# A gated mix of a recurrent-memory attention and a GEGLU block: an eviction, one shared weight slot and the order of some loads are moved

## The chip, the cores and the metric

The kernel runs on one core of one Trainium2 chip. The metric is the device time of one execution in microseconds. A core has five engines that work side by side, each on its own list in order: TensorE (PE, matmuls; its weight loads are shown as PEld), VectorE (DVE), ScalarE (ACT), GpSimd (POOL) and SyncE (SP, which here only issues DMAs). DMA transfers run on 16 DMA engines that all queues share: what SP issues goes through queue q1, what POOL issues through q0, what ACT issues through q10. Matmuls write to eight PSUM banks; ACT or DVE must copy ("evict") a bank to SBUF before its content can be used by PE again.

## The reference

The input x has 2048 rows of 1024. One half (A) is an attention with a recurrent memory: x is cut into 64 segments of 32 rows, and each segment is preceded by 8 memory rows, which are the output of the segment before at its first 8 positions. The other half (B) is a GEGLU block. A gate per row mixes both.

```python
for s in range(n_seg):                       # 64 segments, one after the other
    h = concat([mem, x[:, 32*s:32*s+32]])    # 8 + 32 rows of 1024
    q, k, v = h @ Wq, h @ Wk, h @ Wv         # 32 heads of 128
    p = softmax(where(mask, q @ k.T * scale, -1e9))
    o = (p @ v) @ Wo                         # back to 1024
    mem = o[:, :8]; outs.append(o[:, 8:])
a = concat(outs)
b = (gelu(x @ w_gate) * (x @ w_up)) @ w_down # hidden size 3584
g = sigmoid((x * gate_w).sum(-1))
out = g * a + (1 - g) * b
```

The segments cannot run side by side, since each needs the memory rows of the one before.

## The kernel before, in words

The work is written down once as a list of operations, each with its engine and the tiles it reads and writes; a small class (`_Prog`) works out the semaphore waits from overlaps of these tiles in SBUF and PSUM. So each engine's order is the order in which the operations are listed, and two tiles that lie on the same SBUF bytes make their users wait for one another.

**Weights.** Wq, Wk, Wv and Wo are cut into two halves of 16 heads (u = 0, 1) and eight pieces (i = 0 to 7) of 512 KB each: 64 pieces. SBUF has room for 50 slots. `PAIRS` (L313) names the pieces for which both halves share one slot: two of Wk, two of Wq, four of Wv and six of Wo. A shared slot is loaded anew in each segment. A segment works with one half first (r = 0) and with the other then (r = 1), and the next segment starts with the half that the last one ended with, so a shared slot is loaded once per segment: `spent` (L405) issues the load of the other half from SP as soon as a piece has been used at r = 0. `firsts` (L508) issues the first loads of a half in segment 0. `seq` (L315) gives the order in which the pieces of a half are used. Wo is first read in the layout of the input; as `keep` (L380) it is copied, piece by piece in the first segments, to a scratch tensor wo_scr (one copy per segment, L879), from which later loads come (`load_piece`, L374).

**One segment.** The order of the projections is written out in `HEAD` and `BODY` (L322, L323): first half of Wk, Wq (with the second four steps of the last segment's second Wo half, `("o", 1, 4, 8)`, between them) and Wv; then the second half of Wk and Wq; then Wo at r = 0; then the second half of Wv, then the first four steps of Wo at r = 1. Every projection has eight steps, one piece each (`proj`, L708; Wk, Wq, Wv are the matmuls of L719, Wo at r = 0 those of L735, Wo at r = 1 those of L752). Everything else is hung on these steps by `plan` (L848): `on(m, r, n, f)` lists f just ahead of step n of projection (m, r).

**What hangs there.** `evac` copies a full bank to a stage tile (L613 to L617): kS and qS for the first Wk half and for Wq, pS for the second Wk half. `trans` (L635) turns a stage over with PE transposes (L631) and a DVE copy. `scores` (L644) makes the scores (L647, L653) and the softmax (DVE L659, L660, ACT exponential E of L661, DVE L663 to L672; the last one is the transpose to the tile tAB). `attend` (L674) multiplies the result tAB with the values: the tile vA, evicted from the Wv bank, and vB, read back from a scratch tensor (PE L681, L686). `take` evicts the result to oT. Both halves of a segment have such an attention. For the one with the first half (ua) the eviction of vA hangs ahead of step 3 of the second Wq half (L890), the eviction of the second Wk half to pS ahead of step 1 of that (L900), and `attend` ahead of the Wo stage (L902).

**The memory.** `fold` (L760) adds up a part of the Wo result in DVE and writes the tile a_bf, `next_mem` (L767) turns its memory rows over into hT of the next segment. a_bf is stored to a scratch tensor a_scr from POOL (L938). hT's other rows are loaded by SP (`load_h`, L483).

**Filling work.** The last 8 of the 32 rows of a segment do not go through the chain of hT: their projections are made for four segments at once by `fill` (matmuls L789), in the gaps of other segments. `fill_evac` and `fill_put` (L805, L816) evict, turn over and store them, through the stages kS and oS, to qk_scr or v_scr.

**Tiles on the same bytes.** vA and the stage oS both lie on oT (L300, L305). The stage pS lies on oRc and on a_bf, which follows it (L304, L305). kS lies on kT, qS on qT; tAB and E lie on qT too. So vA's eviction must wait until oT has been read and until a store from oS has landed, and pS's until the store of a_bf has landed.

After the 64 segments the Wo product of the other rows (L960) and the GEGLU block (L1009, L1044, L1063) follow. For these all Wo pieces must be in SBUF, so in the last segment the shared ones are loaded to other slots (`moved`, L386).

Of the kernel before, what the change touches and what calls it, by code (L numbers as in the profile page):

```python
# [210 lines left out]
def bass_gated_mix__memory_aug_recurrent_mem_tr__geglu_ffn__prompt_kernel(  # L211
# [34 lines left out]
    with ExitStack() as es:  # L246
# [26 lines left out]
        def al(name, shape, dt=BF16, at=None):  # L273
            if at is None:
                cur[0] = (cur[0] + 63) // 64 * 64
                t = _T(nc, name, shape, dt, cur[0])
                cur[0] += t.nb
                return t
            return _T(nc, name, shape, dt, at)
# [20 lines left out]
        vA = al("vA", [128, 4, 128], at=oT.off)  # L300
# [9 lines left out]
        NSLOT = (top - cur[0]) // PIECE  # L310


        PAIRS = {"k": (0, 1), "q": (0, 1), "v": (0, 1, 2, 3), "o": (0, 1, 4, 5, 6, 7)}  # L313

        def seq(m, r):  # L315
            p = [i for i in range(8) if i in PAIRS[m]]
            f = [i for i in range(8) if i not in p]
            if (m, r) == ("o", 0):
                return [i + x for i in range(4) for x in (0, 4)]
            return p + f if r == 0 else f + p  # L320

        HEAD = [("k", 0, 0, 4), ("q", 0, 0, 2), ("o", 1, 4, 8), ("q", 0, 2, 4), ("v", 0, 0, 4), ("k", 0, 4, 8), ("q", 0, 4, 8), ("v", 0, 4, 8)]  # L322
# [2 lines left out]
        def at_step(s, m, r, n):  # L325
            return (m, r ^ (s % 2), seq(m, r)[n])
# [10 lines left out]
        for m in "kqvo":  # L337
            for i in range(8):
                if i in PAIRS[m]:
                    hosts.append([(m, 0, i), (m, 1, i)])  # L340
# [10 lines left out]
        for _, e, m, r, n in walk:  # L351
            k = at_step(e, m, r, n)
# [27 lines left out]
        def keep(k):  # L380
# [3 lines left out]

        assert NSEG % 2 == 0
        moved = {("o", 0, i): slots[home[h]] for i, h in zip(PAIRS["o"], (("k", 1, 2), ("k", 1, 3), ("k", 1, 4),  # L386
                                                                          ("q", 1, 6), ("q", 1, 7), ("v", 1, 4)))}
        nlane = [0]
        done = [0] * len(hosts)

# [14 lines left out]
        def spent(k):  # L405
            n = home[k]
            assert uses[n][done[n]] == k
            done[n] += 1
            if done[n] < len(uses[n]) and uses[n][done[n]] != k:
                nk = uses[n][done[n]]  # L410
                if nk in moved and done[n] == len(uses[n]) - 1:
                    load_piece(moved[nk], nk, f"sl{n}")
                else:
                    fetch(n)
# [8 lines left out]
        for g in range(4):  # L423
            q = slice(32 * g, 32 * g + 32)
# [83 lines left out]
        firsts = lambda m, r: [first(at_step(0, m, r, n)) for n in range(8)]  # L508
# [104 lines left out]
        def act_copy(o, i, rd, wr):  # L613
            op("act", lambda e: e.activation(o, i, ACTF.Copy), rd=rd, wr=wr)  # L614
# [6 lines left out]
        def evac(bank, t, how):  # L621
            if how == "both":
                act_copy(t[:, 0:256], PB[bank][:, 0:256], [BK(bank)], [t.r(0, 256)])
                dve_copy(t[:, 256:512], PB[bank][:, 256:512], [BK(bank)], [t.r(256, 512)])
            else:
                cp[how](t[:, :], PB[bank][:, :], [BK(bank)], [t.r()])
# [79 lines left out]
        bank_of = {("k", 0): A0, ("q", 0): A1, ("v", 0): B1, ("k", 1): A0, ("q", 1): A1, ("v", 1): A0}  # L706

        def proj(s, m, r, n):  # L708
            k = at_step(s, m, r, n)
            w = slots[home[k]]  # L710
            if (m, r) == ("o", 1) and s == NSEG - 1:
                w = moved.get(k, w)
            i = k[2]
            if m != "o":
                h, bk = hT[s % 2], bank_of[m, r]

                def f(e):
                    for g in range(4):
                        ins = e.matmul(PB[bk][32 * g:32 * g + 32, :], lhsT=h[:, i, :], rhs=w[:, g * 512:(g + 1) * 512],  # L719
                                       start=(n == 0), stop=(n == 7))  # L720
                    return ins
                op("pe", f, rd=[h.r(32 * i, 32 * i + 32), w.r()], wr=[BK(bk)])
            elif r == 0:
                j = i % 4
                w4 = 4 * LQ
                if n % 2 == 0:
                    wa, wb = slots[home[k]], slots[home[k[0], k[1], i + 4]]
                    na, nb = wa.n, wb.n

                    def f(e):  # L730
                        for hp in range(2):
                            for g in range(4):
                                x = 2 * hp + g // 2
                                c = 512 * x + 256 * (g % 2)
                                ins = e.matmul(PB[XO][32 * g:32 * g + 32, :], lhsT=oT[:, j, x, 0:32],  # L735
                                               rhs=wall[:, na:nb + 1:nb - na, c:c + 256], start=(n == 0 and hp == 0),
                                               stop=False, skip_group_check=True)
                        return ins
                    op("pe", f, rd=[oT.r(j * w4, (j + 1) * w4), wa.r(), wb.r()], wr=[BK(XO)])
                if n % 2:  # L740
                    spent((*k[:2], i - 4))
                    spent(k)
                return
            else:
                j, b = i % 4, i // 4

                def f(e):
                    for hp in range(2):
                        for g in range(4):
                            x = 2 * hp + g // 2  # L750
                            c = 512 * x + 256 * (g % 2)
                            ins = e.matmul(PB[XO][32 * g:32 * g + 32, 256 * b:256 * b + 256], lhsT=oT[:, j, x, 0:32],  # L752
                                           rhs=w[:, c:c + 256], start=False,
                                           stop=(n % 4 == 3 and hp == 1), skip_group_check=True)
                    return ins
                w4 = 4 * LQ
                op("pe", f, rd=[oT.r(j * w4, (j + 1) * w4), w.r()], wr=[BK(XO)])
            spent(k)
# [57 lines left out]
        def fill_put(m, u, G, st):  # L816
            if m == "v":
                return
            st = stage[st]
            turn(st)  # L820
            op("dve", lambda e: e.tensor_copy(st[:, :].rearrange("p (i x c) -> p x i c", i=4, x=16),
                                              PBV[TT][:, 0:512].rearrange("p (x i c) -> p x i c", x=16, i=4)), rd=[BK(TT)], wr=[st.r()])
            m4 = 3 * u if m == "q" else 1 + u
            op("pool", lambda e: e.dma_start(qk_scr[:, 4 * G:4 * G + 4, m4, :], st[:, :].rearrange("p (i y) -> p i y", i=4)),
               rd=[st.r()], wr=[("D", "qk", G, m, u)], lane="fq")
# [22 lines left out]
        def plan(s):  # L848
# [3 lines left out]
            fl = [(m, u, G) for m, u in FILL[s % 4]] if G < NG else []  # L852
# [4 lines left out]
            def on(m, r, n, *fs, s=s):  # L857
                at.setdefault((s, m, r, n), []).extend(fs)

            if s == 0:  # L860
                on("k", 0, 0, lambda: some_x(4, 6))
                on("k", 0, 0, lambda: fill0("k", 0, B0, "k"))
                if NG > 1:
                    on("k", 0, 0, lambda: fill0("k", 0, B1, "o", 1, hR1))
                on("q", 0, 0, lambda: some_x(6, 8))
                on("q", 0, 0, lambda: [load_x(NPX + n) for n in range(4, 8)])
                on("q", 0, 0, lambda: (firsts("k", 1), firsts("q", 1)))
                on("q", 0, 0, lambda: fill0("q", 0, B1, "q"))
                on("v", 0, 0, lambda: some_x(8, 12))
                on("v", 0, 0, lambda: fill0("v", 0, B2, "o"))  # L870
                on("k", 0, 4, lambda: some_x(12, 16))
                on("k", 0, 4, lambda: [do_x(T) or load_x(T + NPX) for T in range(16, NT)])
                on("k", 0, 4, gate)
                on("k", 0, 5, lambda: (firsts("v", 1), firsts("o", 0), firsts("o", 1)))
            if s % 4 == 3 and G < NG:
                on("k", 0, 5, lambda: load_r(G))
            if not last:
                on("k", 0, 4, lambda: load_h(s + 1))
            if 1 <= s <= 2 * len(PAIRS["o"]):  # L879
                on("k", 0, 4, lambda: keep(("o", s % 2, PAIRS["o"][(s - 1) // 2])))  # L880
            on("q", 0, 4, lambda: evac(bank_of["k", 0], stage["k"], "act"))
# [5 lines left out]
            on("v", 0, 6, lambda: trans(qT, "q"))  # L887
            if s == 0:
                on("k", 1, 0, lambda: load_v(0, slice(0, 1)))
            on(*(("k", 1, 1) if s == 0 else ("q", 1, 3)), lambda: evac(bank_of["v", 0], vA, "act"))  # L890
            on("k", 1, 1 if s == 0 else 0, lambda: scores(ua))
            if s == 0:
                on("k", 1, 1, lambda: attend(ua))
# [21 lines left out]
            on("o", 1, 0, some(f1, 8))  # L915
            if fl:
                on("o", 1, 0, lambda: fill_evac(*fl[0], A1, "k"))
                on("o", 1, 2, lambda: fill_put(*fl[0], "k"))
            if not last:
                on("o", 1, 0, lambda: load_qk(s + 1, 0, "sp"))  # L920
            on("o", 1, 0, lambda: op("sp", lambda e: e.dma_start(o_scr[s], oRc[:, :, :].rearrange("p c x -> p (c x)")),
# [186 lines left out]
```

## Time and profile before

| | before |
|---|---|
| median of 3 runs | 2384.8 us (2383.08 to 2384.88) |
| profiled execution | 2371.4 us, span 2369.6 us |
| granted TensorE clock, mean | 0.983 |
| PE busy | 2130.4 us, 90% of the span |
| DMA moved | 639.42 MB, 270 GB/s over the span |
| steady segments (462 to 1687 us) | 25.0 us each, DMA engines busy 0.92, 320 GB/s |
| loads of 512 KB: Wv, Wk, Wq, Wo from wo_scr to wall, Wo from the input to wall | 268, 142, 142, 336, 52 |

The span is cut in 40 slices of 59 us on the page: the first two are the start and segment 0, the segments end in the 29th, then come the Wo product and the GEGLU block. In the views, a line names line and engine, the operation, the tiles (written <- read, buffer numbers left out), the shape and a count. The groups and timeline lines give start and duration, or busy time and mean; in brackets or behind the bar stands how long the engine sat idle before and who released it. The view of waits gives who waited for whom: total us, how often, the longest. The windows view gives each engine's busy time in a stretch, the granted clock, the share of time in which the 16 DMA engines were busy, and GB/s.

### The profile page before, as it was taken

Reading aid. Unit: us, or ns where it says so; the run is one execution under the profiler, and the core shown is the slowest. Engines: PE = TensorE matmul, PEld = TensorE weight load, DVE = VectorE, ACT = ScalarE, POOL = GpSimd, SP = SyncE. Lnnn points to the kernel's source line nnn. Section 1 sums busy time; section 2 is a strip of 40 time slices with the busy share of each in tenths; the row PEclk is TensorE's granted clock in tenths of the full one; section 3 lists DMA queues with packets and bytes.
Section 4 is the critical chain, followed back from the end, with each engine's and each line's share of the span. In section 5 each row is a group of like instructions: output and inputs, shape, how many; then the busy total and the mean of one; then the engine's idle time right before and its main releaser. Section 6 shows DMA issues by size and latency. Waiting matters only on the chain.

```text
span 2369.6 us, 74769 instructions
## 1 busy us (share of the span) xinstructions
PE 2130.4 (90%) x33827; PEld 1054.9 (45%) x33852; DVE 1044.7 (44%) x2438; ACT 519.1 (22%) x985; POOL 432.9 (18%) x821
## 2 busy tenths in 40 slices
PE   4588888989999998999899989988899999999999
PEld 2244444444444444444444444444464444444444
DVE  3344444444444444444444444444415436264463
ACT  1122222222222222222222222222103213032130
POOL 4322222222222222212222222222100000000000
PEclk9799999999999999999999999999999999999999
DMA  9979999989999999999899989999976260713530
GB/s 374 349 267 315 326 321 329 333 309 320 322 316 322 319 323 314 324 324 322 307 321 326 312 318 326 323 318 330 336 249 200 76 217 10 249 53 101 174 99 18
DMA packets 261453, 639.42 MB, mean 270 GB/s; under 512 B 28264, under 2 KB 102760, under 8 KB 261136
## 3 DMA queue, kind: packets, MB, share of 16 engines
q1 hardware_dynamic: 237312, 597.66, 72.4%
q0 software_dynamic: 13888, 26.31, 3.5%
q10 hardware_dynamic: 9936, 10.69, 1.3%
q8 instruction: 266, 4.36, 0.7%
q14 instruction: 51, 0.42, 0.0%
HBM read 596.85 MB, written 37.68 MB: 268 GB/s over the span
## 4 chain that ended last, share of the span: by engine, by line
PE 48%; DMA 29%; DVE 8%; issue 7%; ACT 5%; POOL 3%; ACTq 0%; SPq 0%; POOLq 0%
DMA a_scr<-a_bf 16%; PE pb L1009 14%; DMA wall<-wo_scr 6%; PE pb L719 6%; PE pb L1063 6%; PE pb L735 5%; PE pb L752 3%; PE pb L789 3%; DMA wall<-in_A_Wo_dram 2%; PE pb L960 2%; PE pb L1044 2%; PE pb L631 2%; PE pb L799 2%; ACT pS L614 1%; DMA xr_scr<-xr 1%
## 5 line engine op out<-in xcount | busy, mean ns | idle before, releaser
L719 PE MATMUL pb<-sl,hT 128*32 128x512 bf16 x12288 | 770.1, 382 | 7.2 <-issue 5.0
L719 PEld LDWEIGHTS pb<-sl,hT 128*32 128x32 bf16 x12288 | 342.4, 97 | 273.7 <-DVE hT L776 21.7
L789 PE MATMUL pb<-sl,hR 128*32 128x512 bf16 x3072 | 224.0, 393 | 9.2 <-issue 8.3
L1009 PE MATMUL pb<-xT,wg 128*128 128x512 bf16 x896 | 211.7, 379 | 0.7
L1009 PE MATMUL pb<-xT,wu 128*128 128x512 bf16 x896 | 211.7, 379 | 0.0
L752 PE MATMUL pb<-wall,oT 128*32 128x256 bf16 x4048 | 152.1, 276 | 38.0 <-DMA wall<-wo_scr 16.5
L763 DVE COPY part<-pb 64x256 f32<-64x256 f32 x128 | 54.0, 422 | 265.9 <-PE pb L752 263.4
L735 PE MATMUL pb<-wall,oT 128*32 128x512 bf16 x2048 | 153.1, 396 | 7.6 <-issue 0.2
L614 ACT ACTIVATE kS<-pb 128x512 bf16<-128x512 f32 x127 | 75.8, 597 | 367.9 <-PE pb L719 349.2
L617 DVE CAST oT<-pb 128x160 bf16<-128x160 f32 x382 | 105.5, 318 | 110.3 <-PE pb L686 110.3
L702 POOL COPY oRc<-oT 128x128 bf16<-128x128 bf16 x128 | 96.2, 752 | 313.3 <-DVE oT L617 311.9
L661 ACT ACTIVATE E<-pb 128x320 bf16<-128x320 f32 x128 | 56.0, 437 | 428.1 <-DVE pb L660 428.1
L1063 PE MATMUL pb<-wd,GT 128*128 128x512 bf16 x657 | 144.9, 379 | 2.1 <-DMA wd<-in_B_w_down_dram 1.2
L752 PEld LDWEIGHTS pb<-wall,oT 128*32 128x32 bf16 x4048 | 97.7, 97 | 93.8 <-issue 36.8
L1009 PEld LDWEIGHTS pb<-xT,wg 128*128 128x128 bf16 x896 | 87.0, 98 | 108.1 <-DVE GT L1025 3.7
L1017 ACT ACTIVATE s<-pb 128x512 f32<-128x512 f32 x112 | 66.7, 596 | 311.6 <-PE pb L1009 311.6
L1009 PEld LDWEIGHTS pb<-xT,wu 128*128 128x128 bf16 x896 | 87.5, 98 | 105.9
L1018 DVE SCALAR_TENSOR_TENSOR tp<-s,pb 128x512 f32<-128x512 f32 x112 | 77.0, 687 | 124.1 <-ACT s L1017 123.9
L659 DVE TENSOR_REDUCE st<-pb 128x8 f32<-128x320 f32 x128 | 62.9, 492 | 137.5 <-PE pb L653 137.5
L617 DVE COPY kT<-pb 128x512 bf16<-128x512 bf16 x128 | 53.7, 420 | 156.6 <-PE pb L631 156.6
L828 POOL COPY kT<-qkr 128x128 bf16<-128x128 bf16 x128 | 37.3, 291 | 451.6 <-DVE kT L617 389.3
L789 PEld LDWEIGHTS pb<-sl,hR 128*32 128x32 bf16 x3072 | 84.7, 99 | 68.6 <-issue 20.9
(93 smaller groups left out, 2249.9 us busy)
## 6 DMA issues: line engine op xcount, KB each, us to landing
wall<-wo_scr SPq DMA_DIRECT2D x336, 512.0 KB, 6.9
sl<-in_A_Wv_dram SPq DMA_DIRECT2D x268, 512.0 KB, 10.8
sl<-in_A_Wk_dram SPq DMA_DIRECT2D x142, 512.0 KB, 5.7
sl<-in_A_Wq_dram SPq DMA_DIRECT2D x142, 512.0 KB, 8.4
wd<-in_B_w_down_dram SPq DMA_DIRECT2D x42, 1024.0 KB, 5.5
wall<-in_A_Wo_dram SPq DMA_DIRECT2D x52, 512.0 KB, 7.9
wdF<-in_B_w_down_dram SPq DMA_DIRECT2D x7, 1024.0 KB, 7.7
wo_scr<-wall SPq DMA_DIRECT2D x12, 512.0 KB, 11.9
```

The lines of the kernel that those rows point to most:

```text
L614: op("act", lambda e: e.activation(o, i, ACTF.Copy), rd=rd, wr=wr)
L617: op("dve", lambda e: e.tensor_copy(o, i), rd=rd, wr=wr)
L659: op("dve", lambda e: e.tensor_reduce(nm, sS, AX.X, ALU.max, negate=True), rd=[BK(SS)], wr=[st8.r(0, 8)])
L702: op("pool", lambda e: e.tensor_copy(oRc[:, :, 16 * u:16 * u + 16].rearrange("p c x -> p x c"), oT[:, :, :, 32:40].rearrange("p g j c -> p ...
L719: ins = e.matmul(PB[bk][32 * g:32 * g + 32, :], lhsT=h[:, i, :], rhs=w[:, g * 512:(g + 1) * 512], start=(n == 0), stop=(n == 7))
L735: ins = e.matmul(PB[XO][32 * g:32 * g + 32, :], lhsT=oT[:, j, x, 0:32], rhs=wall[:, na:nb + 1:nb - na, c:c + 256], start=(n == 0 and hp == 0),
L752: ins = e.matmul(PB[XO][32 * g:32 * g + 32, 256 * b:256 * b + 256], lhsT=oT[:, j, x, 0:32], rhs=w[:, c:c + 256], start=False, stop=(n % 4 ...
L789: ins = e.matmul(PB[b][32 * g:32 * g + 32, :], lhsT=h[:, k[2], :], rhs=w[:, g * 512:(g + 1) * 512], start=(n == 0), stop=(n == 7))
L1009: ins = e.matmul(PB[bk][:, 0:FB], lhsT=w[:, kc, cc:cc + 128], rhs=xT[:, :, :, kc, :].rearrange("p t i c -> p (t i) c"), start=(kc == 0), s ...
L1017: op("act", lambda e, hg=hg: e.activation(s1[:, :], hg, ACTF.Square, scale=SQ), rd=[BK(bg)], wr=[s1.r()])
L1018: op("dve", lambda e, hg=hg, t=t: e.scalar_tensor_tensor(out=t[:, :], in0=s1[:, :], scalar=1.0, in1=hg, op0=ALU.add, op1=ALU.mult), rd=[BK ...
L1063: ins = e.matmul(PB[bank[2 * k + hf]][:, :], lhsT=GT[:, j, tb * 128:(tb + 1) * 128], rhs=w[:, jj, hf * 512:(hf + 1) * 512], start=(j == 0) ...
```

## The change

Five edits. (1) `PAIRS`: Wo shares five slots instead of six (piece 7 gets two of its own), Wv five instead of four (piece 4 now shares one). The number of slots and of loads per segment stays. `moved` and the copies to wo_scr follow: five Wo pieces, ten copies. (2) `seq`: the second Wo half is used in the order 2, 3, 0, 1, then 7, 4, 5, 6; before 2, 3, 0, 1, then 4, 5, 6, 7. The second Wv half is used in the order 5, 6, 7, 0, 1, 2, 3, 4; before 4 to 7, then 0 to 3. (3) `proj`: at Wo, r = 0, two pieces are used in each pair of steps, 0 and 4, 1 and 5, 2 and 6, 3 and 7. Their reloads were issued pair by pair: 0, 4, 1, 5, 6, 7. Now they are issued 0 after the first pair, 1, 4, 5 after the second, 6 after the third. (4) The eviction of vA for the first attention is listed ahead of step 4 of the second Wk half instead of step 3 of the second Wq half, so on ACT it stands ahead of pS. (5) In segment 0 the first Wo loads are listed ahead of step 5 of the first Wv half instead of step 5 of the first Wk half, and `fill_put` of the first filling hangs on step 3 of the second Wo half instead of step 2.

```diff
-        PAIRS = {"k": (0, 1), "q": (0, 1), "v": (0, 1, 2, 3), "o": (0, 1, 4, 5, 6, 7)}
+        PAIRS = {"k": (0, 1), "q": (0, 1), "v": (0, 1, 2, 3, 4), "o": (0, 1, 4, 5, 6)}
...
             if (m, r) == ("o", 0):
                 return [i + x for i in range(4) for x in (0, 4)]
+            if m == "o":
+                return sorted(f + p, key=lambda i: i // 4)
             return p + f if r == 0 else f + p
...
         moved = {("o", 0, i): slots[home[h]] for i, h in zip(PAIRS["o"], (("k", 1, 2), ("k", 1, 3), ("k", 1, 4),
-                                                                          ("q", 1, 6), ("q", 1, 7), ("v", 1, 4)))}
+                                                                          ("q", 1, 6), ("q", 1, 7)))}
...
                 if n % 2:
-                    spent((*k[:2], i - 4))
-                    spent(k)
+                    for x in {1: (0,), 3: (1, 4, 5), 5: (2, 6), 7: (3, 7)}[n]:
+                        spent((*k[:2], x))
...
-                on("k", 0, 5, lambda: (firsts("v", 1), firsts("o", 0), firsts("o", 1)))
+                on("k", 0, 5, lambda: firsts("v", 1))
+                on("v", 0, 5, lambda: (firsts("o", 0), firsts("o", 1)))
...
-            on(*(("k", 1, 1) if s == 0 else ("q", 1, 3)), lambda: evac(bank_of["v", 0], vA, "act"))
+            on("k", 1, 1 if s == 0 else 4, lambda: evac(bank_of["v", 0], vA, "act"))
...
-                on("o", 1, 2, lambda: fill_put(*fl[0], "k"))
+                on("o", 1, 3, lambda: fill_put(*fl[0], "k"))
```

## The prediction

> **What bounds the kernel now.** I read the page first, then the sums over the stretch of steady segments, then PE's waits, and last the timeline of one segment (number 31 of 0 to 63).
>
> ```profile
> span 2369.6 us, 74769 instructions
> ...
> PE 2130.4 (90%) x33827; PEld 1054.9 (45%) x33852; DVE 1044.7 (44%) x2438; ACT 519.1 (22%) x985; POOL 432.9 (18%) x821
> ...
> DMA a_scr<-a_bf 16%; PE pb L1009 14%; DMA wall<-wo_scr 6%; PE pb L719 6%; PE pb L1063 6%; PE pb L735 5%; PE pb L752 3%; PE pb L789 3%; DMA wall<-in_A_Wo_dram 2%; PE pb L960 2%; PE pb L1044 2%; PE pb L631 2%; PE pb L799 2%; ACT pS L614 1%; DMA xr_scr<-xr 1%
> ```
>
> ```profile
> core 0: us, PE busy (x) PEld busy (x) DVE busy (x) ACT busy (x) POOL busy (x), PEclk, DMA share, GB/s
> ...
> 462.00:1687.00 1225.00, 1109.27 (x23410) 564.61 (x23413) 564.15 (x1515) 279.23 (x561) 297.18 (x593) 1.00 0.92 320
> ```
>
> The second view holds 49 segments: 25.0 us each, PE busy 22.6, DMA engines 0.92 busy. PE is idle 2.4 us per segment. The first chain entry is no matmul: it is the landing of the store of `a_bf`, for which an eviction waits. PE's waits over the whole span say where that is felt:
>
> ```profile
> PE pb L681 <- ACT vA L614: 46.7, 57, 2.9
> PE pb L681 <- DVE tAB L672: 24.8, 51, 1.7
> PE pb L631 <- ACT kS L614: 21.3, 29, 6.6
> ...
> PE pb L752 <- DMA wall<-wo_scr: 16.5, 28, 1.1
> PE pb L752 <- DMA wall<-in_A_Wo_dram: 12.3, 8, 5.7
> ```
>
> The attention matmuls wait for vA most, then for tAB; the second Wo half waits for its loads. Segment 31:
>
> ```profile
> 906.16 0.46 SPq L485 DMA_DIRECT2D hT<-xq_scr  x1
> 906.31 0.56 POOL L938 DMA_DIRECT2D a_scr<-a_bf  x1
> 910.11 0.44 ACT L661 ACTIVATE E<-pb 128x320 bf16<-128x320 f32 x1 [2.98 <-DVE pb L660]
> 911.93 0.71 DVE L672 STREAM_TRANSPOSE tAB<-pAB 128x512 bf16<-128x512 bf16 x1
> 913.65 0.60 ACT L614 ACTIVATE pS<-pb 128x512 bf16<-128x512 f32 x1 [3.10 <-DMA a_scr<-a_bf]
> 914.14 0.59 ACT L614 ACTIVATE vA<-pb 128x512 bf16<-128x512 f32 x1
> 914.79 0.28 PE L681 MATMUL pb<-tAB,vA 32*128 32x40 bf16 x16 [2.36 <-ACT vA L614]
> 915.03 0.40 PE L631 MATMUL pb<-ident,pS 128*128 128x128 bf16 x4
> 915.55 0.62 PE L735 MATMUL pb<-wall,oT 128*32 128x512 bf16 x8
> 920.55 1.89 PE L719 MATMUL pb<-sl,hT 128*32 128x512 bf16 x32
> ```
>
> ACT takes its work in order. pS (second Wk half) overlies `a_bf`, so it waits until the store issued at 906.31 has landed (913.57 in the trace). vA, whose bank was full before the scores, stands behind pS. tAB has been ready since 912.64; PE starts at 914.79.
>
> **The change part by part.**
>
> **vA ahead of pS.** ACT's idle 3.10 us after E take vA's 0.59, so the attention can start 0.10 after tAB (the trace's shortest such distance), 912.74. What follows does not move as far: the transposes L631 still need pS, which still waits for the store. pS ends at 914.25; a transpose starts 0.14 after its eviction (segment 31: kS ends 906.27, L631 starts 906.41) and the next matmul 0.33 later (906.74), so L735 starts at 914.72 in place of 915.55: 0.83 us, not the 2.36 of the wait. Where tAB is the later one, L735 comes 0.76 after the attention's start, as it does now, and the gain is 0.44 plus (end of pS less end of tAB), between 0 and 0.83. From the trace's times in 61 of the 63 segments after the first: 12 gain 0.83, 35 gain 0.36 in the mean, 14 nothing. 12 x 0.83 + 35 x 0.36 = **22.5 us**. The qS eviction behind pS waits for the attention, which is over by then.
>
> The new wait: vA overlies the stage oS, which in half of the segments is still being stored to qk_scr. vA would stand at ACT's head for it, with pS behind it. In 30 such segments that store lands 0.32 to 1.78 us before that of `a_bf`, 0.50 in the median; pS needs 0.49 behind vA (913.65 to 914.14), so pS slips by 0.17 at most: **+1 us** in all. Bounds: 0, and 30 x 0.8 = 24 if the two landings changed places.
>
> **Wo pair 7 becomes Wv pair 4.** Still 14 loads of 512 KB per segment, but 9 ahead of the Wo stage and 5 in it instead of 8 and 6. Wv piece 4 is issued from SP once its step in the first Wv half is done, behind the hT load, and used in the last step of the second Wv half. In the trace the last loads of a batch land 1.27 to 1.30 apart, earlier ones, beside POOL's small transfers, 1.6 to 2.0; the new one is nearest to the last ones, so it lands 1.27 after hT. From there to the start of the last step are 0.75 us in the mean (10 of 61 already below zero). Bringing that step forward by the first part's gain makes PE wait 7.8 us in all; against the attention behind it 0.22 per segment is covered, since tAB mostly ends 0.22 after vA there, which leaves 4.3. I take **+6**. With 1.64 per load it is 18, with 2.2 it is 42. The lower end is 0.
>
> [...]
>
> **Wo loads in order of use.** Now 0, 4, 1, 5, 6, 7 are fetched while 2, 3, 0, 1 are used first, so piece 1 is third: it lands 9.25 us after the attention's start in the mean and is needed at 9.70, with large scatter, which is the 16.5 us above. Then it is second of Wo and third after hT: 3.92 (hT) + 3 x 1.27 = 7.73, needed at 9.33; in 2 of 61 it would still be late. The 12.3 us from in_A_Wo_dram lie in the first dozen segments, partly behind the copies to wo_scr, which stay for 10 segments instead of 12. I take 14 of 16.5 and 4 of 12.3: **18 us**, with bounds 0 and 28.8. The second group (7, 4, 5, 6) starts with a resident piece; its last takes the sixth place after hT as before. 11 fewer Wo loads come in the input's layout: 0, at most 5 us gained.
>
> **fill_put one step later.** PE waits for kS there 3.7 us in the steady stretch; that goes. But the fold (DVE) stands behind the copy of kS, and moves as much later as PE is earlier: **0**, bounds -2 and +3.
>
> **First Wo loads of segment 0** move on SP behind the new Wv load. One of 16 was issued at 80.5, the other 15 from 88.08 on, where they wait for x's buffers; the Wv step is done at about 85.4, so one load moves 5 us. First use is at 111.79 and that load would still land before 102: 0; if not, one load's 1.3 us. The order of Wv in the second half (5, 6, 7, 0 to 4) reads pieces 0 to 3 one step of 0.24 us earlier, and they land 1.3 us and more ahead of piece 4: 0. The last segment moves five Wo pieces instead of six: 0.
>
> Sum: -22.5 + 1 + 6 - 18 = **-33.5 us**. The profiled execution took 2371.4 us and would take 2338; it lies 13.4 below the median of 2384.8, to which I apply the same difference: **2351 us**, 1.4% less.
>
> **The rivals.**
>
> *Slower: Wv piece 4 comes too late.* It is last in its queue and used last. If a load at that place costs 2.2 us (the spacing in mid-batch in some segments), the wait is 42 us, and the Wo loads behind it lose half of their gain (9): -22.5 + 1 + 42 - 9 = +11.5, **2396**; at 2.7 us it is 68 and 2422. It decides from about 2.1 us per load. Against it: mid-batch spacing goes with POOL's stores, which have landed by then.
>
> *No change: the DMA engines are the bound.* 0.92 busy, 14 loads per segment whatever their order: what PE gains comes back as waits for Wv or Wk loads; **2384**. Against it: at a share of 1 a segment would be 23.0 us, 2 below now, and PE waits more for vA than for any load.
>
> *The store of oS holds pS.* If it landed with or after that of `a_bf`, 30 segments lose 0.8: -33.5 + 24, **2375**.
>
> **How the numbers follow.** The forecast has 0.74, late Wv 0.14, DMA bound 0.09, the oS store 0.03. The forecast's own range is 2327 (all bounds good: -22.5 - 28.8 - 2 - 5) to 2378 (nothing from the Wo order, the Wv wait at 18). 0.2% is 4.8 us, about what a measurement of this kernel can tell from no change. Faster: 0.74 + 0.03; same 0.09; slower 0.14. The range over the cases, 2325 to 2396, takes in the slower rival at its lower price and leaves its worse prices out.
>
> **What would show it.** After the change: the attention matmuls wait for tAB and hardly for vA in the first of the two; L735 starts about 1.07 us after pS where tAB is early, 1.90 before; pS still waits for a_scr; L752's wait for wall falls under 10 us; a wait of the Wv steps (L719) for in_A_Wv of a few us appears; the steady segment takes 24.5 us. Wrong would be: that Wv wait above 40 us, pS released by qk_scr, or the fold moved later by fill_put.

## The result and the profile after

The changed kernel takes 2340.3 us (median of 4 runs, 2337.1 to 2344.3) beside 2383.9 us for the kernel before on the same chip (4 runs, 2372.7 to 2384.9). The ratio is 0.9851, with a 95% interval of 0.9824 to 0.9877: 1.5% less. The forecast was 2351 us, a ratio of 0.986. The profiled execution took 2340.0 us with a span of 2338.2, 31.4 less than the span before. Single runs of one kernel lie up to 17 us from their median, so small differences are read below from ratios over several runs, and places from the traces.

First, from the page of the changed kernel, the chain that ended last by line:

```profile
PE pb L721 16%; PE pb L1012 14%; PE pb L1066 6%; DMA sl<-in_A_Wv_dram 5%; PE pb L754 4%; PE pb L737 4%; DMA qk_scr<-oS 4%; PE pb L791 3%; PE pb L633 3%; PE pb L963 2%; PE pb L801 2%; PE pb L1047 2%; DMA wall<-in_A_Wo_dram 2%; DMA a_scr<-a_bf 2%; DMA wo_scr<-wall 1%
```

(Lines 319 to 873 of the code are now two higher, later ones three: L719 is L721, L752 is L754, L681 is L683.) PE has the same matmuls and is busy 2139.5 us, 9 longer than before, so on balance the gain is idle time. The store of `a_bf` has gone from 16% of the chain to 2%, though pS still waits for it, as segment 31 below shows. Two DMAs stand there instead: Wv loads, 5%, and the store of oS to qk_scr, 4%, for which vA now waits at the head of ACT (29.9 us over the span, 29 times).

Next the sums by stage, segments 1 to 12 ("early") and the 49 steady ones behind them, each counted from its first attention, first of the kernel before, then after. Columns: stretch, length, busy time of each engine with its instructions, granted clock, share of DMA time, GB/s.

```profile
137.70:462.70 325.00, 282.74 (x5768) 138.53 (x5772) 138.61 (x372) 68.90 (x138) 73.93 (x147) 0.96 0.92 315
462.70:1687.20 1224.50, 1109.41 (x23423) 564.70 (x23423) 564.15 (x1515) 278.64 (x559) 297.18 (x593) 1.00 0.92 320
```

```profile
137.20:444.80 307.60, 276.22 (x5763) 137.26 (x5764) 138.85 (x372) 69.21 (x139) 74.28 (x147) 0.99 0.94 330
444.80:1653.20 1208.40, 1118.21 (x23411) 566.96 (x23411) 565.14 (x1515) 279.17 (x560) 298.54 (x593) 0.99 0.92 325
```

The 12 early segments give 17.4 us, the 49 steady ones 16.1. The start is 0.4 shorter, and what follows the segments gives back some 2.5. In the steady part PE's idle time (length less busy) falls from 115.1 to 90.2, and 8.8 us of that are lost again to a busier PE, at a granted clock of 0.99 in place of 1.00. In the early part idle time falls from 42.3 to 31.4 and PE is busy 6.5 us less, as the clock rises from 0.96 to 0.99.

PE's waits after, over the whole span (who waited for whom: total us, how often, the longest):

```profile
PE pb L683 <- DVE tAB L674: 14.9, 33, 1.6
...
PE pb L721 <- DMA sl<-in_A_Wv_dram: 11.0, 10, 2.4
...
PE pb L754 <- DMA wall<-in_A_Wo_dram: 8.6, 7, 2.5
...
PE pb L683 <- ACT vA L616: 3.9, 9, 0.7
```

The wait for vA is 3.9 where it was 46.7. The waits for wall have fallen from 28.8 to under 10. A Wv wait of 11.0 is new. Segment 31, its ACT instructions, the end of its softmax on DVE, and its PE instructions (start and duration; idle time before in brackets):

```profile
886.07 0.44 ACT L663 ACTIVATE E<-pb 128x320 bf16<-128x320 f32 x1 [2.98 <-DVE pb L662]
886.41 0.59 ACT L616 ACTIVATE vA<-pb 128x512 bf16<-128x512 f32 x1
888.65 0.60 ACT L616 ACTIVATE pS<-pb 128x512 bf16<-128x512 f32 x1 [1.66 <-PE pb L721]
```

```profile
887.90 0.71 DVE L674 STREAM_TRANSPOSE tAB<-pAB 128x512 bf16<-128x512 bf16 x1
```

```profile
888.71 0.28 PE L683 MATMUL pb<-tAB,vA 32*128 32x40 bf16 x16 [0.25 <-issue]
888.82 0.21 PE L688 MATMUL pb<-tAB,vB 32*128 32x64 bf16 x4
889.30 0.40 PE L633 MATMUL pb<-ident,pS 128*128 128x128 bf16 x4 [0.28 <-ACT pS L616]
889.63 0.62 PE L737 MATMUL pb<-wall,oT 128*32 128x512 bf16 x8
```

vA follows E at once. tAB ends at 888.61 (887.90 and 0.71) and the attention starts 0.10 later, no longer behind pS. L737 starts 0.98 us after pS does, where it took 1.90.

The releasers in the brackets mislead here. pS starts 0.07 us behind the landing of the store of `a_bf`, as it did before (913.65 and 913.57): so it does in 52 of the 63 segments after the first, in 61 before. The attention starts 0.10 behind tAB in 52 of them, in 16 before, and this wait too is shown as "issue". L737 comes 0.98 behind pS in 12 segments only, where tAB is early; the median is 1.59, before 1.90.

### The profile page after: what moved, and what is told of

Its sections match the earlier page's. It is cut to its first block, busy times and chain, and to the rows that moved or that the text cites. A ratio compares the mean times of both kernels' runs of the same rounds, so it can differ in the third digit from the quotient of the medians.

```text
span 2338.2 us, 74819 instructions
## 1 busy us (share of the span) xinstructions
PE 2139.5 (92%) x33852; PEld 1058.2 (45%) x33852; DVE 1046.2 (45%) x2438; ACT 519.5 (22%) x985; POOL 434.7 (19%) x821
## 4 chain that ended last, share of the span: by engine, by line
PE 62%; DMA 19%; DVE 8%; issue 6%; ACT 3%; POOL 2%; SPq 0%; ACTq 0%; POOLq 0%
PE pb L721 16%; PE pb L1012 14%; PE pb L1066 6%; DMA sl<-in_A_Wv_dram 5%; PE pb L754 4%; PE pb L737 4%; DMA qk_scr<-oS 4%; PE pb L791 3%; PE pb L633 3%; PE pb L963 2%; PE pb L801 2%; PE pb L1047 2%; DMA wall<-in_A_Wo_dram 2%; DMA a_scr<-a_bf 2%; DMA wo_scr<-wall 1%
## 5 line engine op out<-in xcount | busy, mean ns | idle before, releaser
L721 PE MATMUL pb<-sl,hT 128*32 128x512 bf16 x12288 | 781.2, 382 | 26.3 <-issue 13.6
L721 PEld LDWEIGHTS pb<-sl,hT 128*32 128x32 bf16 x12288 | 343.7, 96 | 305.4 <-issue 33.0
L754 PE MATMUL pb<-wall,oT 128*32 128x256 bf16 x4056 | 150.7, 278 | 16.9 <-DMA wall<-in_A_Wo_dram 8.6
L737 PE MATMUL pb<-wall,oT 128*32 128x512 bf16 x2048 | 151.0, 391 | 5.9
L754 PEld LDWEIGHTS pb<-wall,oT 128*32 128x32 bf16 x4056 | 102.9, 98 | 64.1 <-ACT oT L616 24.1
```

## The experiments

Three sets ran, each on one chip beside the kernel before (median 2374.9 us of 23 runs, 2380.5 of 17, 2380.8 of 18): c1 and e1 to e3, then e4 to e7, then c2 and e8 to e10. The ratios are to the kernel before in the same set. The second set did not hold the changed kernel, so its runs are set beside the changed kernel's ratios in the two others. A difference of two ratios carries about 10 us either way.

The table is worked out from the traces, as a map to what follows; the second and third group of columns are PE's idle time ahead of the attention matmuls (L681 before), of the second Wo half (L752) and of the Wk, Wq and Wv steps (L719), whoever ended it. Each row is one run: that of the kernel before is 13 us faster than the median in its first table, that of c1 is 6 faster than its median, those of e2, e6 and e8 are 12, 8 and 7 slower than theirs.

| kernel | early: length | attention | Wo, 2nd half | W steps | steady: length | PE busy | attention | Wo, 2nd half | W steps |
|---|---|---|---|---|---|---|---|---|---|
| before | 325.0 | 14.8 | 18.2 | 2.0 | 1224.5 | 1109.4 | 56.8 | 17.7 | 5.2 |
| e1, vA alone | 325.4 | 6.9 | 18.5 | 7.4 | 1213.0 | 1113.9 | 32.6 | 11.9 | 12.0 |
| e2, load order alone | 321.8 | 12.1 | 16.8 | 6.2 | 1247.0 | 1118.1 | 53.7 | 30.2 | 7.5 |
| e6, all but load order | 330.0 | 6.6 | 18.1 | 12.5 | 1234.8 | 1122.2 | 31.6 | 30.1 | 9.1 |
| e8, slots and order | 310.2 | 9.9 | 5.3 | 8.9 | 1232.0 | 1118.3 | 50.9 | 5.2 | 14.7 |
| e9, fill_put alone | 318.2 | 12.9 | 17.2 | 2.6 | 1228.0 | 1123.1 | 50.2 | 19.3 | 5.4 |
| e3, all but vA | 307.1 | 6.8 | 8.3 | 5.4 | 1223.5 | 1116.0 | 49.0 | 6.0 | 14.1 |
| after | 307.6 | 3.9 | 8.6 | 12.6 | 1208.4 | 1118.2 | 28.7 | 6.2 | 13.4 |
| after again (c1) | 309.7 | 5.0 | 5.1 | 9.7 | 1200.0 | 1111.9 | 28.2 | 6.9 | 16.4 |
| after again (c2) | 307.9 | 5.5 | 9.6 | 9.3 | 1205.0 | 1117.6 | 30.9 | 6.9 | 16.2 |

**The changed kernel again, beside the first set** (c1, no edit).

> The changed kernel once more, on the chip of the three next runs, as their measure. 30 to 45 us below the kernel before; steady segments of 24.6 us, 25.0 before.

2338.0 us, ratio 0.9851 [0.9825, 0.9878]: 35 us, as in the first comparison. Its trace shows how far one trace differs from the next: 8.3 us between the two spans of the changed kernel (2329.9 and 2338.2), 6 of them in PE's busy time in the steady part.

**vA alone** (e1), in the kernel before.

```diff
-            on(*(("k", 1, 1) if s == 0 else ("q", 1, 3)), lambda: evac(bank_of["v", 0], vA, "act"))
+            on("k", 1, 1 if s == 0 else 4, lambda: evac(bank_of["v", 0], vA, "act"))
```

> The kernel before with the move of vA alone. The forecast's first part: the first attention of a segment starts 0.10 us after tAB, L735 about 1.0 us after pS at the earliest (1.90 before), and the time falls by 22.5 us. Rival, the DMA engines are the bound: the waits for wall and for Wv or Wk loads grow by what the attention gains, and the time falls by less than 5 us.

2367.6 us, ratio 0.9967 [0.9943, 0.9991]: 8 us gained, between 2 and 14. PE's waits for Wo loads over the span:

```profile
PE pb L752 <- DMA wall<-wo_scr: 14.5, 20, 1.9
PE pb L752 <- DMA wall<-in_A_Wo_dram: 12.2, 6, 3.7
```

They are little less than before (16.5 and 12.3). PE waits longest for tAB now, 25.1 us, and hardly for vA. Yet the early segments take 325.4 us as before. There the attention starts 0.55 us sooner after its segment's first step than before, but from it to the second Wo half 0.38 more pass, and 0.21 more from there to the next segment: the loads come no sooner. That of Wo piece 1 lands 10.93 us behind the attention's start there, where it was 10.41. Some of the missing gain is chance: PE idles 4.6 us more than before in this part in gaps with no releaser (the last section). The steady segments gain 11.5.

**The order of the Wo loads alone** (e2), in the kernel before.

```diff
-                    spent((*k[:2], i - 4))
-                    spent(k)
+                    for x in {1: (0,), 3: (1, 4, 5), 5: (2, 6), 7: (3, 7)}[n]:
+                        spent((*k[:2], x))
```

> The kernel before with the reloads of Wo issued in order of use alone (piece 0 after the first pair of steps, 1, 4, 5 after the second, then 6, then 7); slots and everything else as before. If the order is what removes the waits of L752, including the one of 5.67 us in segment 1, and the stretches at half the TensorE clock that follow it, then the time falls by 14 to 20 us, most of it before segment 13. Rival, the move of a load out of the Wo batch does it: the waits stay within 5 us of before and the time falls by at most 5 us.

2382.0 us, ratio 1.0019 [0.9996, 1.0042]: no gain. PE's waits for Wo loads:

```profile
PE pb L752 <- DMA wall<-wo_scr: 21.7, 26, 1.5
...
PE pb L752 <- DMA wall<-in_A_Wo_dram: 14.1, 14, 2.5
```

The waits for wall have not gone, they have moved within the stage. Ahead of the step that uses piece 1 PE's idle time falls from 21.0 us to 3.9 (early and steady together), and ahead of the last step it rises from 6.4 to 25.1. In steady segments piece 1 lands 8.18 us after the attention's start in place of 9.10, but the last piece at 13.98 in place of 13.24. With only one load issued after the first pair of steps, a gap opens behind it: the next one lands 2.75 us later, where 1.3 to 1.8 is usual.

**All but the load order** (e6): slots exchanged, vA and fill_put moved, reloads pair by pair.

```diff
-                    for x in {1: (0,), 3: (1, 4, 5), 5: (2, 6), 7: (3, 7)}[n]:
-                        spent((*k[:2], x))
+                    spent((*k[:2], i - 4))
+                    spent(k)
```

> The changed kernel with the reloads of Wo issued pair by pair again (0, 4, then 1, 5, then 6). Piece 1 is then third of Wo and fourth after hT. If the order matters in steady segments too, L752 waits 10 to 20 us more for wall and the time grows by 10 to 20 us; if it only matters in the first dozen segments, growth is under 10 us and lies before segment 13.

2384.3 us, ratio 1.0020 [0.9998, 1.0042]: the whole gain of the change is gone, although vA stands ahead of pS. PE's longest wait is now:

```profile
PE pb L754 <- DMA wall<-wo_scr: 34.3, 37, 2.4
```

The extra Wv load now stands ahead of the Wo loads, so piece 1 is the fourth load behind hT; in steady segments it lands 9.88 us after the attention's start. PE's idle time ahead of its step is 44.3 us, and none is left ahead of the last. Against the changed kernel the Wo stage costs 24 us more in the steady part and 9.5 more in the early one.

**Slots and order, without vA and fill_put** (e8; the later first Wo loads of segment 0 stay, too). The two edits to `on(...)` of vA and fill_put are undone in the changed kernel.

```diff
-            on("k", 1, 1 if s == 0 else 4, lambda: evac(bank_of["v", 0], vA, "act"))
+            on(*(("k", 1, 1) if s == 0 else ("q", 1, 3)), lambda: evac(bank_of["v", 0], vA, "act"))
...
-                on("o", 1, 3, lambda: fill_put(*fl[0], "k"))
+                on("o", 1, 2, lambda: fill_put(*fl[0], "k"))
```

> The changed kernel without the move of vA and without that of the filling's turn: only the exchange of the slot and the two orders are left. If the parts add up (about 14 us for vA, 11 for the turn by the runs so far), 8 to 16 us below the kernel before, with the gain ahead of segment 13. If these two are worth less than their single runs said, 17 to 25 us below.

2363.1 us, ratio 0.9916 [0.9885, 0.9947]: 20 us gained, between 13 and 27. The wait for vA is there as before (40.3 us). One of the two without the other (the order in e2, the slots beside vA and fill_put in e6) only moves the wait from one Wo piece to another; together both pieces are in time, 4.9 us are left ahead of piece 1 and the last piece together, where it was 27.4. In this trace all of the gain lies in the early segments (325.0 to 310.2). That holds beyond one trace: the nine traces with both edits take 305.4 to 312.9 us there, the five without one of them 318.2 to 330.0. In the steady ones of e8's trace the Wo stage loses 12.5 us of waiting too, but PE is busy 8.9 us longer and waits 9.5 more at the W steps, 3.6 of it for Wv.

**All but vA** (e3): vA is put back behind pS in the changed kernel (the first pair of lines of the diff above).

> The changed kernel with vA's eviction back behind pS. If the parts add up, 20 to 23 us above the changed kernel. If the two parts compete for the same slack (Wv piece 4 then has more time), the loss is smaller, 10 to 15 us.

2352.0 us, ratio 0.9905 [0.9876, 0.9933], against 0.9851 for the changed kernel in the same set: vA is worth 13 us here, between 4 and 22. Its wait is back (39.2 us in all). The early segments are as long without the vA move (307.1) as with it (307.6). The steady ones are 0.31 to 0.47 us longer each (24.97 against 24.66, 24.50 and 24.59 in three traces of the changed kernel); the forecast made it 22.5 / 61 = 0.37.

**The copies to wo_scr behind the Wv load** (e4). The early Wv wait has a cause that the forecast had missed: in the early segments piece 4 lands 2.5 us after hT, not 1.25, since the copy of a Wo piece to wo_scr (`keep`) stands between the two in SP's queue. Here it is issued behind the Wv load:

```diff
-                on("k", 0, 4, lambda: keep(("o", s % 2, PAIRS["o"][(s - 1) // 2])))
+                on("v", 0, 5, lambda: keep(("o", s % 2, PAIRS["o"][(s - 1) // 2])))
```

> The changed kernel with the copy of a Wo piece to wo_scr issued behind the load of Wv piece 4 instead of ahead of it (segments 1 to 10). In these segments the piece lands 2.5 us after hT with the copy ahead, 1.25 without it, and PE waits 9.0 us for it between 137 and 445 us. If the copy is the cause, that wait falls under 2 us and the time by 5 to 9 us. Rival: the copy then lands later and holds the reload of the piece that it reads; the wait for wall grows by as much and the time stays within 3 us.

2344.4 us, ratio 0.9859 [0.9831, 0.9888], the same as the changed kernel's. PE's waits in the early segments:

```profile
PE pb L754 <- DMA wall<-in_A_Wo_dram: 8.6, 9, 1.3
...
PE pb L754 <- DMA wall<-wo_scr: 3.7, 4, 1.8
```

The Wv wait is off this list (9.0 us in the changed kernel). 3.7 us of it have come back as a wait for Wo loads, which now stand behind the copy, and the early segments are no shorter: 310.2 us, against 307.6 to 309.7. That speaks for the amount which SP's queue has to move there, and against the order, as what bounds them.

**Piece 4 used four steps earlier** (e5). The second Wv half reads piece 4 ahead of pieces 0 to 3, so that the load that lands last is used fourth and not eighth.

```diff
+            if (m, r) == ("v", 1):
+                return f + p[4:] + p[:4]
```

> The changed kernel with Wv piece 4 used as the fourth of the second half (5, 6, 7, 4, 0 to 3) instead of the last: it is needed four steps, 0.94 us, earlier, all else equal. This is the price of the slower rival. If the landing of this piece bounds the segment as soon as its slack (0.75 us in the mean before the change) is used up, the wait of the Wv steps grows to 35 to 55 us and the time by 25 to 50 us. If the attention behind it and later gaps take it up, by less than 10 us.

2355.6 us, ratio 0.9901 [0.9873, 0.9928]: 12 to 21 us slower than the changed kernel (0.9851 and 0.9812 in other sets). PE's longest wait:

```profile
PE pb L723 <- DMA sl<-in_A_Wv_dram: 38.6, 40, 3.3
```

The slower rival's mechanism exists and can be priced: 27.6 us more waiting for Wv, of which 8.2 are covered because PE then waits less for tAB (14.9 to 6.7). By these medians a late Wv piece costs in time about a half to three quarters of what it shows as waiting. So it is piece 4's place at the end of the second Wv half, on which the forecast's +6 rests, that keeps the new load harmless.

**fill_put put back** (e7), in the changed kernel (the second pair of lines in the diff of e8).

> The changed kernel with the turn of the filling's stage back ahead of step 2 of the second Wo half. The forecast gives this part nothing: within 3 us of the changed kernel, with PE waiting some 4 us more for kS. Rival: the wait of PE is on the path and the time grows by 4 us or more.

2355.7 us, ratio 0.9899 [0.9871, 0.9927]: again 11 to 21 us slower than the changed kernel, each with some 10 us either way.

**fill_put alone** (e9), in the kernel before.

```diff
-                on("o", 1, 2, lambda: fill_put(*fl[0], "k"))
+                on("o", 1, 3, lambda: fill_put(*fl[0], "k"))
```

> The kernel before with the filling's turn one step later alone. Forecast: 0, between 2 gained and 3 lost. If the first fold after it really starts 0.11 us and the next segment 0.1 to 0.2 us earlier, as between the traces with and without it, then in some 30 segments 3 to 5 us are gained. As much as 11 us would need another path.

2378.9 us, ratio 0.9984 [0.9961, 1.0006]: 4 us, not told from nothing. The two together: the place shows the wait for kS (3.7 us in the steady part) going and 1.2 to 2.3 us of waiting for `a_bf` coming back, and the next segment starts 0.1 to 0.2 us sooner in some 30 segments, 3 to 5 us. That accounts for e9. It does not account for e7. Its trace shows 8 us more waiting at the transposes L633 (11.9 in all: pS 6.1, kS 3.9, no releaser 1.9), and 7 to 15 us more in gaps behind transfers of q8 in the steady part than three traces of the changed kernel (the last section).

Two more pairs of runs bear on this. With both load edits but vA behind pS, fill_put is worth 3 us (e3 against e8, 0.9905 and 0.9916). With them but without fill_put, vA is worth 4 (e7 against e8, 0.9899 and 0.9916). Either alone gives 3 or 4 us beyond e8, both together 15 to 25. Whether that is more than the scatter of such differences, and what would make the two help each other, stays open.

**The changed kernel again, beside the third set** (c2, no edit).

> The changed kernel on the chip of the three next runs, as their measure: 30 to 45 us below the kernel before.

2338.0 us, ratio 0.9812 [0.9779, 0.9844]: 45 us. The median is that of the first set; it is the kernel before that is slower on this chip.

**The second scores earlier** (e10). The changed kernel's largest wait is for tAB, ahead of the second attention of a segment. Its scores are listed two Wo steps earlier:

```diff
-            on("o", 0, 6, lambda: scores(ub))
+            on("o", 0, 4, lambda: scores(ub))
```

> A step beyond the changed kernel: the scores of the second attention stand ahead of step 4 of the Wo stage instead of step 6. There PE waits 0.36 us for tAB in two segments of three, and vA's eviction is over 0.22 us before tAB. If that wait is on the path, tAB comes 0.3 us earlier, vA then ends the wait, and 0.22 us in some 40 segments are 8 to 10 us. Rival: PE reaches the scores before qT and waits there for as long; within 3 us of the changed kernel.

2338.6 us, ratio 0.9813 [0.9777, 0.985], the same as the changed kernel's in this set. tAB ends PE's wait ahead of the second attention in 1 of 49 segments, against 33 in the changed kernel (c2), and the idle time ahead of the second attention falls from 0.30 us to 0.10 in the mean, 10 us over the 49 segments. None of it arrives in the median. Part comes back at the second Wo half (9.5 us in the steady part, against 6.2 to 6.9), which is now reached earlier than its loads land; where the rest goes was not found.

## Why the prediction came out right, point by point

**The total** was forecast at 33.5 us less and measured as 35 in the first comparison and in the first set, and 45 in the third set. The forecast's own case happened; its split over the parts was wrong in three places. That the total came within 2 us in the first two is in part luck: vA gave less than forecast, the loads gave 8 more, and with fill_put comes a gain where none was forecast. The upper end of the forecast's own range is 2381 by its own terms (-22.5 + 1 + 18), not 2378; nothing else hangs on it.

**vA ahead of pS, 22.5 us.** The mechanism is as described: the attention starts 0.10 after tAB, L737 0.98 after pS where tAB is early (1.07 was said), in 12 segments as forecast; pS starts 0.07 behind the landing of its store in 52 of 63; the wait for vA falls from 46.7 to 3.9. What failed is the count of segments. "35 gain 0.36 in the mean", "12 gain 0.83" was summed over all 61 segments, as if PE were the bound in each. In the 12 early ones it is the loads that are, and there e1 and e3 show no gain. In the 49 others 0.31 to 0.47 us per segment are gained. Measured: 8 us alone (2 to 14), 13 beside all other edits (4 to 22), 4 without fill_put. The new wait of vA for the store of oS (**+1**) shows in the chain as 4%: vA starts 0.02 behind that landing in 30 segments, and pS is held by 0.19 at most, 0.8 us in all, as forecast (0.17 and 1).

**Wv piece 4, +6.** Right in the steady part: it lands 1.25 us after hT (1.27 was said), 419 GB/s for its 512 KB, the wait is 2.1 us, 2.7 in c1. Missed in the early part: "the last loads of a batch land 1.27 to 1.30 apart" left out that the copy to wo_scr lies in between, so 9.0 us are waited there (4.6 in c1). At 11.0 in all the term is 5 us too small as waiting, but e4 shows that without the copy there the Wo loads take the same time.

**Wo loads in order of use, -18.** Priced as a term of its own beside +6 for the slot, it failed: alone it gains nothing (e2), and without it the slot exchange takes back all that the rest gives (e6). There is one term for both, -20 us measured (e8, 13 to 27), against -12 forecast. The working "second of Wo and third after hT" was true only of the kernel with both edits, which is why the total suffered little. Piece 1 then landed 8.4 us behind the attention's start (e8 and the changed kernel) and not 7.73, since the two Wo loads came 1.4 to 1.9 apart and not 1.27; that is still ahead of the 9.33 forecast for its step. Its place was wrong too: "14 of 16.5" in the steady part and "4 of 12.3" in the early one. The steady waits did go (11.4 us for wo_scr to 0.3), but the gain in time lies in the early segments. There the waits at the second Wo half went from 18.2 us to 8.6 in the changed kernel and to 5.3 in e8, and the clock recovered.

**fill_put, 0 with bounds -2 to +3.** Too narrow: 4 us alone, 3 beside the load edits, 11 to 21 when taken out of the whole, the larger part unexplained. The parts do not simply add: the loads at 20, vA at 13 and fill_put at 11 to 21 make 44 to 54, above the measured 35 to 45, since what vA and fill_put may give only together is counted in both of the last two. Added one after the other, 20 (e8), 3 (e3) and 13 (the changed kernel) make 36.

**First Wo loads, last segment, 0.** The time up to segment 1 is 0.4 us shorter and that behind the segments about 2.5 longer, neither more than traces of one kernel differ by.

**The rivals.** *DMA engines the bound*: falls in the steady part. The DMA share is 0.92 as before and the rate rises from 320 to 325 GB/s, with PE's idle time 25 us lower. In the early part it holds by halves: there vA gains nothing, and moving the copy only moves the wait (e4). *Late Wv piece*: it is real (e5), but with the load used last the steady wait is a few us. *The store of oS holds pS*: it does so for 0.8 us over the span.

## What to carry to other kernels

Which weights share a slot and in which order their loads are issued is one decision: price it by writing down, for the kernel with all edits, when each piece lands and when its step comes, and look at the piece that is last after the change as well as the one that was late before. Ahead of summing a gain per segment, sort the segments by what bounds them: in the early ones here, where loads do, vA's earlier eviction gave no time (325.4 us in e1 beside 325.0, 307.6 after beside 307.1 in e3). ACT ran vA and pS in the order in which they are listed in all 63 segments after the first, pS ahead before and vA ahead after, so an eviction that waits for a store goes behind those that are ready: here that took 35 us off one wait (e3 against the changed kernel) and 13 us off the time. The last section adds two things to look for: PE's busy share in each 3.413 us, and the transfers of the queue q8.

## What the runs showed that was not expected

**Half clock after short gaps.** In segment 1 of the kernel before PE waits twice for a Wo load, and the granted clock falls to half. First PE's timeline, then the stretch with the granted clock in the third column from the right:

```profile
147.46 0.40 PE L752 MATMUL pb<-wall,oT 128*32 128x256 bf16 x8 [1.25 <-DMA wall<-in_A_Wo_dram]
153.53 0.62 PE L752 MATMUL pb<-wall,oT 128*32 128x256 bf16 x8 [5.67 <-DMA wall<-in_A_Wo_dram]
```

```profile
148.60:158.80 10.20, 5.27 (x54) 2.16 (x58) 1.02 (x3) 0.00 (x0) 0.25 (x1) 0.50 0.64 214
```

The clock is at half for 10.2 us, which is 3 x 3.4, and then full at once. The early segments before hold 27.3 us of such stretches, all multiples of 3.4; those of the changed kernel hold 3.4, 10.2 and 0 in three traces. That is where PE's 6.5 us less of busy time in the early part come from: a wait for a load is paid a second time in slower matmuls. In the stretch above 16 matmuls of L789 take 1.95 and 1.90 us (at 153.91 and 156.01); at 237.42, at full clock, 16 take 1.05. Other traces agree: PE is busy 275.9 to 277.2 us in this part in the three with no half clock there, 282.7 to 284.5 in the three with a mean clock of 0.96. But it does not take a long gap. In the changed kernel, at 690:

```profile
692.40 0.20 PE L688 MATMUL pb<-tAB,vB 32*128 32x64 bf16 x3 [2.34 <-issue]
```

```profile
690.00:693.70 3.70, 1.22 (x24) 0.49 (x17) 1.05 (x5) 0.60 (x1) 0.10 (x1) 1.00 1.03 405
693.70:697.10 3.40, 3.40 (x61) 1.29 (x65) 0.93 (x4) 0.00 (x0) 1.13 (x3) 0.51 0.82 263
```

One gap of 2.34 us, in a stretch of 3.7 us with PE busy for 1.22, is followed by 3.4 us at 0.51. In the clock records of these two traces every stretch at half clock is 3413 ns long, or two, three or five times that, but for one at the very end of each record. So a gap shorter than one such length can be followed by a whole one at half clock.

All such stretches of a trace start on one grid of 3.413 us. Cut along it into windows, the 14 traces of this case hold 6081 windows at full clock between segment 1 and 1650 us, and 96 of them are followed by one at half clock. In these 96 PE was busy for 0.12 to 0.62 of the window, with a longest gap of 0.71 to 2.85 us. All 33 windows with a busy share under 0.40 were followed by half clock, none of the 5828 above 0.62; between the two both happen. That it hangs on the sum of the gaps in a window rather than on one gap is the author's reading of these counts.

**Gaps behind the transfers of q8.** In each trace PE idles 20 to 49 us of the steady part in pieces of up to 3.7 us that end with no releaser ("issue"): 25.5 us before and 42.5, 36.8 and 34.1 in three traces of the changed kernel. Of these three, 7.2, 5.4 and 6.9 us end 0.10 us behind tAB, as in segment 31, and are waits for tAB. The others lie at changing places. The page of the changed kernel has a queue that bears on them (packets, MB, share of 16 engines):

```profile
q8 instruction: 266, 4.36, 0.8%
```

These are 266 transfers of 16 KB; PE has 68252 recorded instructions, 257 for each. In the 14 traces 597 gaps of the steady parts remain, and 596 of them end 1.0 to 1.8 us after such a transfer has ended; at random places it would be one in eight. The gap of 2.34 us above is one: the transfer ends at 690.95, PE goes on at 692.40. Such a gap follows about every fourth of the 184 transfers of a steady part. That PE waits there for its next instructions is the author's reading of the queue's name and of these numbers; no view shows it. What sets these transfers apart from the others is open.

Without the waits for tAB these gaps sum to 24.9 us before and 35.3, 31.4 and 27.2 in three traces of the changed kernel. They are as large as the effects looked for here and, with 8.1 us between these three, part of the scatter between runs. The clock is another part: of the 18 runs of the kernel before in the third set the longest, 2398.0 us, has the lowest mean clock, 0.974, and the shortest, 2367.6, the highest, 0.983.
